# Two transformer layers on one core: scaled copies of V made for eight heads at a time, weights kept for the last queries, one residual sum in the tail moved to TensorE, and a new order of the work

## The chip, the core and the metric

The kernel runs on one core of one Trainium2 chip. The metric is the time of one execution on the device in microseconds (us). Engines are named as in the profile: PE is TensorE, ACT is ScalarE, DVE is VectorE, POOL is GpSimd, and SP is SyncE, which here only issues DMAs.

## What is computed

Two layers on x, 2048 tokens by 512 features, bfloat16. Each layer is attention (32 heads of 16) and a feed-forward block (hidden width 1792), both with a layer norm without weights in front and a residual sum behind.

```python
x = x + _A_ref(_layernorm(x), A_wqkv, A_wo)      # softmax(q k^T / 4) v, then @ wo
x = x + _B_ref(_layernorm(x), B_w1, ..., B_b2)   # gelu(h @ w1 + b1) @ w2 + b2
x = x + _A_ref(_layernorm(x), A_wqkv, A_wo)      # the same weights again
x = x + _B_ref(_layernorm(x), B_w1, ..., B_b2)
```

## The kernel before

**Cells and passes.** Queries are cut into four chunks of 512 columns (`segs`; in the second layer the last chunk is cut into two segments of 256), keys into 16 tiles of 128 (`kt`). A *cell* is one head, one key tile and 512 queries (or two heads with 256 queries each): one score matmul on PE (L1336), the exponential of a 128x512 PSUM bank, and a product with V (L1851). There are 4096 cells, 2048 per layer. A *pass* (`passes`) is one query segment, four heads (eight for the segments of 256) and a range of key tiles; over all 16 tiles it has 64 cells. Layer 2 begins with passes over key tiles 0 to 11 alone, since the last four tiles are not there yet.

**Two ways to an exponential.** Most cells go to ACT, two or three banks in one instruction (`exps`, L1787), and their result is one operand of V's product. Cells whose key tile is in `KD[l]` (five of the 16 tiles of a layer) may go to DVE instead: `dfirst` (L1493) makes an integer from the score that, read as bfloat16, is a rough exponential, and `dchain` (L1610 on POOL, L1615 and L1621 on DVE) makes three shifted versions of it. All four are multiplied with V and three scaled copies of V, tile `VC`, and the sum is a good exponential. `vcopies` (L1267, POOL) makes the copies, for all 32 heads of a key tile at a time, 15 instructions per layer; those of the second layer start when the first pass of that layer is reached.

**The layer norm and the feed-forward block.** `ln` and `ln_tile` compute statistics on DVE, the reciprocal root on POOL (L751), the normed tile on POOL (L767, into a ring `XLN` of two buffers), and SP transposes it by DMA (L771) into `XF`, for W1, or `XP`, for the next layer's projections. `hpair` is W1 (L638), `gelu` runs on ACT (L1077), `ytile` is W2. `wo` is the output projection; its result is added to x on DVE (L960). Weights stream through a ring `WR` of four buffers (`wloads`, `wload`, SP, L1012). `wlate` loads four W1 pieces of the very last segment into room that layer 1's keys had. For the last query chunk, W2 stays in the room of Q (`lent_q`).

**Lent room.** Exponentials wait for PE in the units `pt`: a ring of 15 and, when they are free, the rooms of K, Q, G, XP and V. The room's old keys are given as written each time a unit in it is written again (`pkeys`, `alias`; `over` for the buffers of DVE).

**The order.** Nothing of the order is written by hand. While the kernel is built, `_Sched` plays all threads against durations written in the code and emits, for each engine, a fixed list of instructions with semaphore waits. `_Op` carries an engine, a duration, what it reads and writes, and a priority (small is first). Rows of settings (`ROWS`), one for each of 160 stretches of the cells (`PIECES`), steer the choices. Where the plan has PE idle it puts in matmuls without use (`filler`, L1324); an empty column of a V product gets a product with zeros (L1859). On the chip each engine goes through its list in order and cannot change it.

The planner's line that decides between ready operations of one engine:

```python
ch = min(nowc, key=lambda c: (self._prio(c[0].op), c[0].seq))
```

Of the kernel before, what the change touches and what calls it, by code (L numbers as in the profile page):

```python
# [23 lines left out]
PT_RING = 15  # L24
# [3 lines left out]
W_MORE = 4  # L28
XT = 8
XLN_RING = 2  # L30
# [15 lines left out]
KD = ((4, 5, 6, 7, 8), (0, 1, 2, 12, 13))  # L46
# [9 lines left out]
QUEUE = 4  # L56
NAMES = ("SWAP", "SLACK", "LATE", "TOL", "BACKLOG", "OPENING", "TAIL", "PVP", "PTURG", "DUURG", "DULOW", "DWIDE", "RWIDE", "PTLOW", "FPRIO", "MID",
         "EVAC", "ROUNDS", "ALONE", "AHEAD", "PSHIFT", "QUEUE", "SOLO", "BACK", "SIDE", "BOTH", "DMAX", "GMAX", "PMORE", "DUMORE",)
ROWS = (
# [568 lines left out]
class _Plan:  # L628
# [336 lines left out]
    def wdone(self, piece, r):  # L965
        self.wleft[piece] -= 1
        if self.wleft[piece] == 0:
            yield ("rel", "w", r)
# [994 lines left out]
```

## Time and profile before

| what | value |
|---|---|
| median of 3 runs | 1505.63 us (1504.88 to 1507.16) |
| the profiled execution | 1504.69 us, span of its instructions 1502.9 us, so 1.8 us lie around the span |
| busy | ACT 1454.3 us (97%), PE 1443.9 (96%), DVE 1346.3 (90%), POOL 918.4 (61%) |
| granted TensorE clock | 1.00 throughout |
| exponentials on ACT (L1787) | 984 instructions over two banks, 342 over three |
| cells on DVE (L1493) | 1102 |
| scaled copies (L1267) | 30, 19.8 us of POOL, mean 662 ns |
| last exponential ends | 1471.5 us, that is 31.4 us before the end of the span |

A busy share is an average. PE's contains matmuls without use, and its durations overlap, since a matmul starts before the one ahead of it has ended. ACT's instructions overlap a little as well: two in a row start closer to each other than one lasts.

### The profile page before, as it was taken

The numbers are of one execution on the slowest core, as the hardware profiler recorded it, in microseconds if no ns is written. First come the engines' busy times: TensorE is split into PE (matmuls) and PEld (weight loads), VectorE is DVE, ScalarE is ACT, GpSimd is POOL, SyncE is SP. The second block draws the span as 40 slices with busy tenths as digits, with TensorE's granted clock in tenths as the row PEclk, the third lists the DMA queues.
The fourth block names the chain that finished last, engine by engine and source line by source line (L and its number), as shares of the span: only waits on it lengthen the run. The fifth ranks groups of instructions, "written<-read, shape, count | busy, mean of one in ns | idle before, by whom it ended". The sixth has DMA issues, their size and how long they took to land.

```text
span 1502.9 us, 46561 instructions
## 1 busy us (share of the span) xinstructions
PE 1443.9 (96%) x20102; PEld 440.9 (29%) x20102; DVE 1346.3 (90%) x2343; ACT 1454.3 (97%) x1385; POOL 918.4 (61%) x975
## 2 busy tenths in 40 slices
PE   8999999999999999999999999989999999999998
PEld 2222222222222222222222222222222222344345
DVE  5589999989999899998889788899989998999894
ACT  7999999999999999999889999999999999999994
POOL 4547766786655565645654456676766776676550
PEclk9999999999999999999999999999999999999999
DMA  5200001153021342114331441001144114411433
GB/s 148 51 1 2 1 12 34 36 156 92 23 51 37 107 111 64 47 37 127 93 99 41 144 113 30 9 2 44 30 118 130 29 37 135 146 26 44 136 100 108
DMA packets 145048, 103.41 MB, mean 69 GB/s; under 512 B 37069, under 2 KB 143822, under 8 KB 144846
## 3 DMA queue, kind: packets, MB, share of 16 engines
q1 hardware_dynamic: 144846, 100.44, 23.7%
q8 instruction: 161, 2.64, 0.7%
q14 instruction: 41, 0.34, 0.1%
HBM read 88.61 MB, written 4.19 MB: 62 GB/s over the span
## 4 chain that ended last, share of the span: by engine, by line
ACT 43%; PE 39%; DVE 16%; issue 1%; DMA 0%; POOL 0%; SPq 0%; ACTq 0%; DVEq 0%
ACT pt L1787 34%; PE ps L1851 13%; PE ps L638 13%; PE ps L1336 13%; DVE du L1493 6%; DVE du L1615 3%; ACT g L1077 3%; ACT kt L1787 2%; ACT v L1787 1%; ACT g L1787 1%; DVE kt L1493 1%; DVE v L1493 1%; ACT xp L1787 1%; PE ps L1324 1%; DVE stats L744 1%
## 5 line engine op out<-in xcount | busy, mean ns | idle before, releaser
L1787 ACT ACTIVATE pt<-ps 128x1024 bf16<-128x1024 f32 (+1 forms) x1122 | 1166.3, 1164 | 16.8 <-PE ps L1336 12.5
L1610 POOL TENSOR_SCALAR du<-du 128x1024 uint16<-128x1024 uint16 x430 | 446.9, 1043 | 300.7 <-DVE du L1493 159.0
L1493 DVE TENSOR_SCALAR du<-ps 128x512 uint16<-128x512 f32 x855 | 566.2, 682 | 55.4 <-PE ps L1336 50.6
L1336 PE MATMUL ps<-qp,kt 32*128 32x512 bf16 x4096 | 547.8, 384 | 27.6 <-ACT pt L1787 13.4
L1851 PE MATMUL ps<-pt,v 128*17 128x512 bf16 (+1 forms) x2795 | 384.4, 359 | 6.4 <-ACT pt L1787 1.6
L1851 PE MATMUL ps<-du,vc 128*17 128x512 bf16 (+1 forms) x2883 | 347.4, 357 | 2.5 <-DVE du L1615 1.6
L1336 PEld LDWEIGHTS ps<-qp,kt 32*128 32x128 bf16 x4096 | 140.9, 91 | 577.3 <-ACT pt L1787 172.4
L1615 DVE TENSOR_SCALAR du<-du 128x2048 uint16<-128x2048 uint16 (+1 forms) x313 | 226.1, 738 | 9.4 <-POOL du L1610 9.2
L1851 PE MATMUL ps<-du,v 128*17 128x512 bf16 (+1 forms) x961 | 159.2, 359 | 5.1 <-DVE du L1615 1.2
L1859 PE MATMUL ps<-vc,zero 128*17 128x512 bf16 x733 | 151.2, 381 | 0.0
L638 PE MATMUL ps<-xf,wr 128*32 128x512 bf16 (+1 forms) x1888 | 128.8, 365 | 1.0 <-DVE g L1056 0.9
L1623 POOL TENSOR_SCALAR du<-du 128x1024 uint16<-128x1024 uint16 x117 | 122.7, 1049 | 8.1 <-DVE du L1621 5.1
L1851 PEld LDWEIGHTS ps<-pt,v 128*17 128x17 bf16 x2795 | 93.6, 88 | 101.8 <-issue 63.9
L1493 DVE TENSOR_SCALAR kt<-ps 128x512 uint16<-128x512 f32 x167 | 113.6, 682 | 8.8 <-PE ps L1336 6.1
L638 PE MATMUL ps<-wr,g 128*32 128x512 bf16 x1600 | 119.8, 383 | 1.5 <-DVE du L1493 0.5
L1610 POOL TENSOR_SCALAR kt<-kt 128x1024 uint16<-128x1024 uint16 x84 | 87.7, 1045 | 52.4 <-DVE du L1615 25.6
L1284 POOL TENSOR_SCALAR qp<-q,mask 128x512 bf16<-128x512 bf16 (+1 forms) x91 | 64.0, 703 | 87.4 <-PE ps L1336 41.3
L1851 PEld LDWEIGHTS ps<-du,vc 128*17 128x17 bf16 x2883 | 94.2, 89 | 74.8 <-issue 45.0
L1851 PE MATMUL ps<-kt,vc 128*17 128x512 bf16 (+1 forms) x621 | 103.2, 339 | 0.1
L1787 ACT ACTIVATE kt<-ps 128x1024 bf16<-128x1024 f32 (+1 forms) x77 | 94.4, 1242 | 1.1 <-PE ps L1336 0.3
L1851 PE MATMUL ps<-kt,v 128*17 128x512 bf16 (+1 forms) x393 | 92.2, 360 | 1.4 <-DVE v L909 0.4
L1056 DVE TENSOR_SCALAR g<-ps,hb1t 128x512 bf16<-128x512 f32 (+1 forms) x112 | 78.9, 708 | 5.5 <-PE ps L638 5.0
(107 smaller groups left out, 1635.1 us busy)
## 6 DMA issues: line engine op xcount, KB each, us to landing
wr<-in_B_w_dram SPq DMA_DIRECT2D x256, 256.0 KB, 2.9
wr<-in_A_wqkv_dram SPq DMA_DIRECT2D x24, 256.0 KB, 2.9
wr<-in_A_wo_dram SPq DMA_DIRECT2D x18, 256.0 KB, 3.2
x<-in_A_x_dram SPq DMA_DIRECT2D x7, 512.0 KB, 4.2
kept<-x SPq DMA_DIRECT2D x4, 512.0 KB, 3.9
x<-kept SPq DMA_DIRECT2D x4, 512.0 KB, 4.1
out_dram<-x SPq DMA_DIRECT2D x16, 128.0 KB, 2.3
g<-in_A_wqkv_dram SPq DMA_DIRECT2D x3, 512.0 KB, 6.0
```

The source lines that it names most:

```text
L638: return [lambda e, a=a: e.matmul(out[32 * a:32 * a + 32, :], lhsT=lhsT[:, 32 * a:32 * a + 32], rhs=rhs, start=start, stop=stop, tile_posi ...
L1056: yield _Op("dve", 0.21 + n / 966, lambda e, fc=fc, pb=pb: e.tensor_scalar(T["G"][:, fc, q], pb, T["HB1T"][:, fc:fc + 1], None, op0=ALU.ad ...
L1077: lambda e, g=g: e.activation(out=g, in_=g, func=ACT.Gelu_apprx_tanh), reads=gk, writes=gk, prio=2)
L1284: yield _Op("pool", 0.27 + 0.42 * w / 512, lambda e, s=s, q=q, i=i, t=t, w=w: e.tensor_scalar(T["QP"][:, s, w * i:w * i + w], q, T["MASK"] ...
L1336: return (lambda e: e.matmul(o, lhsT=lhsT, rhs=rhs, start=True, stop=True, tile_position=(32 * a, 0)), ["K%d.%d.%d" % (l, gb, kt // 4), "Q ...
L1493: yield _Op("dve", 0.682, lambda e: e.tensor_scalar(u, self.bank(b), E_SCALE, E_BIAS, op0=ALU.mult, op1=ALU.add), reads=["B.%d" % b], writ ...
L1610: one = _Op("pool", 0.15 + 0.45 * n, lambda e, a=a, b=b: e.tensor_scalar(b, a, float(SHIFT), 1.0, op0=ALU.add, op1=ALU.mult), reads=key[0] ...
L1615: two = _Op("dve", 0.152 + 0.266 * n, lambda e: e.tensor_scalar(U[:, 2:4, 0:n, :], U[:, 0:2, 0:n, :], 2 * SHIFT, None, op0=ALU.add), reads ...
L1623: more = _Op("pool", 0.15 + 0.45 * n, lambda e, a=a, c=c: e.tensor_scalar(c, a, float(2 * SHIFT), 1.0, op0=ALU.add, op1=ALU.mult), reads=k ...
L1787: yield _Op("act", 0.065 + 0.4267 * n, lambda e, src=src, dst=dst: e.activation(out=dst, in_=src, func=ACT.Exp, scale=0.25), reads=["B.%d" ...
L1851: op.fns.append(lambda e, o=o, lhsT=q[0][0][m], rhs=q[0][1][:, n * m:n * m + n], a=a, st=st, sp=sp: e.matmul(o, lhsT=lhsT, rhs=rhs, start= ...
L1859: op.fns.append(lambda e, o=self.bank(b)[32 * a:32 * a + 17, :], rhs=rhs, a=a, st=not begun[a], sp=end: e.matmul(o, lhsT=T["ZERO"][:, 0:17 ...
```

## The change

- `KD` of the second layer is (1, 4, 7, 10, 13) in place of (0, 1, 2, 12, 13), so that it has one step. `VC` becomes two buffers, each for eight heads and five key tiles. A *visit* is a run of passes with the same eight heads, segment and key tiles; for each, `vcopies` issues three instructions over all its key tiles. A buffer is written again when the products of the visit that used it are past.
- The room set free goes to `PT_RING` (15 to 21) and `XLN_RING` (2 to 4).
- XP is no longer lent to exponentials. It becomes two weight buffers, in which Wo stays for the last three segments (`wkeep`); the four late W1 pieces are asked for 80 cells before the end (`WSOON`).
- W2 kept in the room of Q serves the last two query chunks, not only the last.
- Old keys of lent room are given as written at the first write alone (`once`).
- In the last segment x is added by a matmul with the identity into the bank of `wo`; the statistics read that bank, and ACT copies it to x. The bias of W2 is put into the bank first there.
- The norm into XP has priority 3.5 (`LNQ`), where the copies have 4 and it had 7. DMA transposes get priority 1.
- `GMAX` is gone, there are 61 rows of settings and another `PIECES`, and a stretch ends at a rounded place. Matmuls without use read `B2row` in place of `VC`.

```diff
-KD = ((4, 5, 6, 7, 8), (0, 1, 2, 12, 13))
+KD = ((4, 5, 6, 7, 8), (1, 4, 7, 10, 13))
...
+        T["WR"] += [T["XP"][:, 2 * i:2 * i + 2, :].rearrange("p c q -> p (c q)") for i in range(W_KEEP)]
-        T["VC"] = sb([128, NKD, 3, H * 17], BF16, "vc")
+        T["VC"] = sb([128, 2, 3, NKD, H // 4 * 17], BF16, "vc")
...
     def wo(self, l, seg, t):
+        if (l, seg) == (NL - 1, self.segs[l][-1]):
+            yield ("need", "exps")
+            b = yield ("acq", "misc")
+            yield self.resid(b, t, True, False)
...
+        if last:
+            yield ("give", ("xready", t, 2 * l + 1), b)
+            yield ("need", ("st", t))
+            yield _Op("act", 0.48, lambda e: e.copy(T["X"][:, t % XT, :], pb), ...)
+            yield ("give", ("xback", t))
+            return
+    def resid(self, b, t, start, stop):
+        return _Op("pe", MM, self.quads(self.bank(b), self.T["IDENT"], self.T["X"][:, t % XT, :], start, stop), ...)
...
     def wlate(self, todo):
+        yield ("cond", lambda: self.scored >= self.total - WSOON)
...
+    def wkeep(self, todo):
+        for i, (piece, (src, n), uses) in enumerate(todo):
+            if i < W_KEEP:
+                yield from self.wload(piece, src, n, uses, W_RING + W_MORE + i, ["XP.%d" % j for j in range(4)] if i == 0 else [])
+            else:
+                self.wleft[piece] = uses
+                yield ("give", ("w",) + piece, W_RING + W_MORE + i % W_KEEP)
...
     def ytile(self, l, seg, t):
-        tail = l == NL - 1 and seg[0] == self.NQ - 1
+        tail = l == NL - 1 and seg[0] >= self.NQ - 2
+        if l == NL - 1 and seg[0] == self.NQ - 1:
+            yield ("need", "exps")
...
-                yield ("spawn", self.ln(ts, xp, pk, LNP, gate=("pfree",) + prev if prev else None), LNP)
+                yield ("spawn", self.ln(ts, xp, pk, LNQ, gate=("pfree",) + prev if prev else None), LNQ)
...
     def vcopies(self):
+        for v in range(len(first)):
+            l, seg, g, kts = self.pas[first[v]][:4]
+            js = [j for j, kt in enumerate(KD[l]) if kt in kts]
+            if js:
+                if used[v % 2] is not None:
+                    yield ("cond", lambda pi=first[used[v % 2] + 1]: self.pv >= pi)
...
+                for i, w in enumerate(VW):
+                    yield _Op("pool", 0.15 + 0.133 * len(js), lambda e, i=i, w=w, v=v, js=js, src=src: e.tensor_scalar(
+                        T["VC"][:, v % 2, i, js[0]:js[-1] + 1, :], src, w, 1.0, op0=ALU.mult, op1=ALU.mult), ...)
...
     def dfirst(self, pair, j, b):
-                  reads=["B.%d" % b], writes=["DU.%d.0.%d" % (pair["du"], j)] + self.over(pair["du"]))
+                  reads=["B.%d" % b], writes=["DU.%d.0.%d" % (pair["du"], j)] + self.once.pop(("du", pair["du"], j), []))
...
     def exps(self):
-                reads=["B.%d" % b for b in self.slots[sl][:n]], writes=[k for r in run for k in self.pkeys(r)])
+                reads=["B.%d" % b for b in self.slots[sl][:n]], writes=[k for r in run for k in self.pkeys(r) + self.once.pop(r, [])])
```

How many instructions of each kind the two programs hold, counted in their built lists:

| | before | after |
|---|---|---|
| ACT exponentials over 1, 2 and 3 banks | 0, 984, 342 | 1, 976, 349 |
| cells on DVE | 1102 | 1096 |
| POOL shifted versions (two cells each; L1610, L1623) | 708 | 668 |
| DVE shifted versions, double (L1615) and single (L1621) | 388, 160 | 422, 123 |
| POOL scaled copies: 544 wide; 680; 136 | 30; 0; 0 | 18; 90; 18 |
| PE products with V over 512 columns, the zeros included | 7569 | 7477 |
| PE matmuls without use (128x512 bank, four at a time) | 516 | 516 |
| PE matmuls behind the last score, of W1's 256-column kind | 368 | 224 |
| DMA loads of W2 pieces and of Wo pieces into WR | 197, 18 | 169, 10 (and 2 into XP) |

More of the change, by code (lines that the diff above doesn't have):

```diff
@@ L742, in ln @@
         for t in tiles:
-            yield ("need", ("xready", t, self.phase[t // 4]))
-            yield _Op("dve", 0.66, lambda e, t=t: e.bn_stats(T["STATS"][:, t, :], T["X"][:, t % XT, :]),
-                      reads=["X.%d" % (t % XT)], writes=["ST.%d" % t])
+            b = yield ("need", ("xready", t, self.phase[t // 4]))
+            src, key = (self.bank(b), "B.%d" % b) if quick and self.phase[t // 4] else (T["X"][:, t % XT, :], "X.%d" % (t % XT))
+            yield _Op("dve", 0.66, lambda e, t=t, src=src: e.bn_stats(T["STATS"][:, t, :], src), reads=[key], writes=["ST.%d" % t], prio=prio)
+            if key[0] == "B":
+                yield ("give", ("st", t))
+                yield ("need", ("xback", t))
+                yield ("rel", "misc", b)
             yield _Op("dve", 0.17, lambda e, t=t: e.bn_aggr(T["MV"][:, t, :], T["STATS"][:, t, :]),
@@ L984, in first, with kept @@
             return [((l, seg, "O", j), rows(hbm["wo"], 256 * j, 0, D), seg[2] // 128) for j in range(2)]
+        def kept(l, seg):
+            return l == NL - 1 and seg[0] > 0
+        yield ("spawn", self.wkeep([x for o in order if kept(*o) for x in first(*o)]), 3)
         out = first(*order[0])
@@ L988, in wloads @@
             todo = [((l, seg, "1", p), cols(hbm["w1"], 256 * p), 2) for p in range(NFC // 2)]
-            tail = l == NL - 1 and seg[0] == self.NQ - 1
-            if not tail:
+            if l == NL - 1 and seg[0] == self.NQ - 2:
+                p = NFC // 2 - 1
+                todo.append(((l, self.segs[l][-1], "2", p), rows(hbm["w2"], 256 * p, 0, D), 8))
+            elif l < NL - 1 or seg[0] < self.NQ - 1:
                 todo += [((l, seg, "2", (t, p)), rows(hbm["w2"], 256 * p, 0, D), 1) for t in self.tiles(seg) for p in range(NFC // 2)]
             elif i == len(order) - 1:
-                p = NFC // 2 - 1
-                todo.insert(0, ((l, seg, "2", p), rows(hbm["w2"], 256 * p, 0, D), 4))
-                late = todo[1:1 + W_MORE]
-                del todo[1:1 + W_MORE]
-            if i < len(order) - 1:
+                late = todo[:W_MORE]
+                del todo[:W_MORE]
+            if i < len(order) - 1 and not kept(*order[i + 1]):
                 todo += first(*order[i + 1])
@@ L1004, in wloads @@
         for i, (piece, (src, n), uses) in enumerate(out):
-            if i == len(out) - (NFC // 2 + 1 - W_MORE):
-                yield ("spawn", self.wlate(late), 3)
+            if i == 0:
+                yield ("spawn", self.wlate([x for x in late]), 3)
             w = yield ("acq", "w")
@@ L1019, in wlate @@
         for i, (piece, (src, n), uses) in enumerate(todo):
-            yield from self.wload(piece, src, n, uses, W_RING + i, over)
+            yield from self.wload(piece, src, n, uses, W_RING + i, over if i == 0 else [])
+    def wkeep(self, todo):
+        for c in range(self.NQ):
+            for kind in "KVQ":
+                for i in range(4):
+                    yield ("need", (kind, 1, 4 * c + i if kind == "V" else i, c))
+        for i, (piece, (src, n), uses) in enumerate(todo):
[4 more added lines that the diff above has]
+                yield ("give", ("w",) + piece, W_RING + W_MORE + i % W_KEEP)
     def gkeys(self, seg, fs):
@@ L1082, in ytile @@
         T = self.T
-        tail = l == NL - 1 and seg[0] == self.NQ - 1
+        tail = l == NL - 1 and seg[0] >= self.NQ - 2
         last = NFC // 2 - 1
-        for p in range(1 if tail else NFC // 2):
-            yield ("need", ("g", l, seg, p))
+        if l == NL - 1 and seg[0] == self.NQ - 1:
+            yield ("need", "exps")
+        else:
+            for p in range(1 if tail else NFC // 2):
+                yield ("need", ("g", l, seg, p))
         b = None if tail else (yield ("need", ("w", l, seg, "2", (t, 0))))
@@ L1101, in ytile @@
             for j in range(2):
-                fns += self.quads(pb, T["G"][:, 2 * p + j, q], ws[j], p + j == 0, False)
-            if p == last:
+                fns += self.quads(pb, T["G"][:, 2 * p + j, q], ws[j], not early and p + j == 0, early and 2 * p + j == NFC - 1)
+            if p == last and not early:
                 fns += self.quads(pb, T["ONES1"][:, :], T["B2row"][:, :], False, True)
@@ L1234, in setup_attention @@
                 self.pvleft[(pi, a)] = len(kts)
+        self.visit = []
+        for pi, (l, seg, g, kts, part, final) in enumerate(self.pas):
+            new = pi == 0 or self.pas[pi - 1][0:2] != (l, seg) or self.pas[pi - 1][3:] != (kts, part, final) or self.heads(*self.pas[pi - 1][1:3])[0] != self.heads(seg, g)[0]
+            self.visit.append(self.visit[-1] + new if pi else 0)
         self.total, self.scored, self.nd, self.pa, self.pv = n, 0, 0, 0, 0
@@ L1250, in setup_attention @@
                      ["K0.%d.%d" % (i, c) for i in (0, 1) for c in range(self.NQ)] + ["PART1.%d" % g for g in range(4)]]
+        for du in range(self.own, len(self.cap)):
+            for j in range(self.cap[du]):
+                self.once[("du", du, j)] = self.over(du)
         self.lead = [min(pi for pi, p in enumerate(self.pas) if p[0] == l) for l in range(NL)]
@@ L1668, in setup_units @@
             for i in range(NDC):
-                self.alias[lo + i] = ["K1.%d.%d" % (i, c)] + ["XL.%d" % t for t in range(4 * c, 4 * c + 4)]
+                self.alias[lo + i] = ["K1.%d.%d" % (i, c)]
+                self.once[lo + i] = ["XL.%d" % t for t in range(4 * c, 4 * c + 4)]
         self.qblocks = len(self.blocks)
@@ L1722, in lent_g @@
                     yield ("need", ("xready", t, 2 * l + 2))
-    def lent_xp(self, lo, hi):
-        for c in range(self.NQ):
-            for kind in "KVQ":
-                for i in range(4):
-                    yield ("need", (kind, 1, 4 * c + i if kind == "V" else i, c))
-        for u in range(lo, hi):
-            yield ("rel", "pt", u)
     def lent(self, c, lo, hi):
```

88 lines of the change are left out of this document (50 added, 38 removed), and 119 rows, old and new, of tables (PIECES, ROWS).

## Prediction

> **What bounds the kernel now.** I read the page's busy line first, then ACT's waits, then stretches of time, then the two places where ACT stands still.
>
> ```profile
> span 1502.9 us, 46561 instructions
> PE 1443.9 (96%) x20102; PEld 440.9 (29%) x20102; DVE 1346.3 (90%) x2343; ACT 1454.3 (97%) x1385; POOL 918.4 (61%) x975
> ...
> PEld ps L1336 <- ACT pt L1787: 172.4, 383, 1.7
> ...
> ACT pt L1787 <- PE ps L1336: 12.5, 14, 7.8
> ```
>
> ACT and PE are both nearly full. The lower lines are of the table of waits (waiter, releaser, total us, times, longest): PE's weight loads for scores waited 172.4 us for ACT's exponentials to leave a bank, ACT waited 12.5 us for scores. So ACT sets the pace, with PE little behind. The table of stretches says where ACT is not busy (columns: PE, PEld, DVE, ACT, POOL busy, then clock and DMA):
>
> ```profile
> 100.00:700.00 600.00, 581.54 (x7541) 160.00 (x7537) 574.86 (x981) 596.10 (x566) 384.32 (x396) 1.00 0.20 56
> 700.00:800.00 100.00, 95.81 (x1312) 28.59 (x1309) 88.31 (x157) 90.30 (x88) 61.08 (x69) 1.00 0.33 91
> 800.00:1450.00 650.00, 624.32 (x8947) 194.67 (x8944) 593.65 (x1023) 644.89 (x606) 417.59 (x433) 1.00 0.26 75
> ...
> 1471.00:1503.00 32.00, 27.86 (x694) 18.59 (x682) 12.33 (x31) 11.89 (x19) 1.23 (x2) 1.00 0.37 110
> ```
>
> Outside the opening ACT misses 9.7 us between 700 and 800, some 9 us in 1250 us elsewhere, and it is a guest in the tail, where PE has 27.9 of 32. Three terms follow: ACT's work, the hole at 746, the tail.
>
> **ACT's work: +2.5 us.** From the list of built instructions: 8 exponentials fewer over two banks, 7 more over three, one over a single bank (six cells went from DVE to ACT). By the rows of shapes these take 1066 and 1493 ns; the copy of one bank (L834) 649 to 674, which I take as 0.6. -8 x 1.066 + 7 x 1.493 + 0.6 = +2.5. All are on ACT's path.
>
> **The hole at the layers' border: -6.1 us.** Timelines of ACT, POOL and SP there (start, us until the last of the row ends, instructions, [idle before]):
>
> ```profile
> 737.92 8.22 ACT L1787 ACTIVATE pt<-ps 128x1536 bf16<-128x1536 f32 x7
> 753.97 6.69 ACT L1787 ACTIVATE pt<-ps 128x1024 bf16<-128x1024 f32 x7 [7.82 <-PE ps L1336]
> ...
> 738.06 1.51 POOL L767 TENSOR_SCALAR xln<-x,rstd,nmr 128x512 bf16<-128x512 bf16 x2
> 739.80 1.37 POOL L1267 TENSOR_SCALAR vc<-v 128x544 bf16<-128x544 bf16 x2 [0.23 <-PE ps L1859]
> 741.53 4.98 POOL L1267 TENSOR_SCALAR vc<-v 128x544 bf16<-128x544 bf16 x7 [0.36 <-DVE ott L923]
> 746.61 1.52 POOL L767 TENSOR_SCALAR xln<-x,rstd,nmr 128x512 bf16<-128x512 bf16 x2
> ...
> 738.85 11.06 SPq L771 DMA_TRANSPOSE xp<-xln  x4
> ```
>
> ACT ends an exponential at 746.15 and waits 7.82 us for a score. That score needs a K tile whose projection PE starts at 751.64, when the transposes into XP are there; those need four normed tiles on POOL. POOL makes two, then nine scaled copies, then the other two at 746.61; `XLN` has two buffers. In the new list POOL's four L767 of this place stand together, directly behind the root, with four buffers, and the copies behind them. So the second pair is ready at 739.6 + 1.5 = 741.1 instead of 748.1. Two transposes take about 2.5 us of SP (the row of two at 753.78 says 2.50): the first pair is through at 741.3, the second at 743.8 instead of 749.9, 6.1 us earlier. Projection, cast, score and exponential move along, the first exponential to 747.9. 1.7 us of the hole stay. Next late is then PE: it has to put the output projections of the last segment (L638, 741.5 to 749.4) around it, in whose gaps it now runs 60 matmuls without use (L1324). In the new list PE has 16 and 4 of those around this border where it had 72 and 8: a sign that the gap is gone, not proof. Ends: 0 (another input of that score was as late) and -7.8.
>
> **The tail: -3.5 us.** The last exponential ends at 1471.46, the span 31.4 us later. Rows of PE and the last one of DVE:
>
> ```profile
> 1472.80 3.02 PE L638 MATMUL ps<-xf,wr 128*32 128x256 bf16 x104
> 1475.64 1.47 PE L638 MATMUL ps<-q,g 128*32 128x512 bf16 x24
> ...
> 1500.06 0.69 DVE L1109 TENSOR_TENSOR x<-x,ps 128x512 bf16<-128x512 bf16 x1 [1.25 <-PE ps L638]
> ```
>
> PE is the chain here from 1472.8 to 1500.0. 104 matmuls of W1 (256 columns) take 2.84 us until the next row, 27 ns each; of 512 columns, 24 take 1.29, 54 ns each. Behind the last score the new list has 144 fewer of the first kind: W1 of the segment before the last is now done ahead. -144 x 0.0273 = -3.9. Eight identity matmuls are new: +0.4. W2, Wo, the bias and W1 of the last segment are as many as before. The sum left, 22 us, can be packed like this: products with V end about 0.9 us after the last exponential (1.5 today, with 0.9 of W1 among them); DVE's norm of the heads takes 0.72 + 0.24 + 0.49 + 0.43 by its rows, so Wo starts at 3.0; the first half of gelu, which has 1.28 of table load and 1.70 ahead of it, is there at 3.0 too. From there 21.1 us of PE, 0.3 to 1 of waits, 0.75 for the last sum and 2.15 from there to the end of the span as today: 27.3 to 28, against 31.4. I take 27.9. The new cover: today W1 hides the norm and gelu; when it is gone PE idles about 1.1 us, which is in this sum. The old sum of x and `wo` on DVE (0.68 a tile) leaves the chain to the statistics; it was off PE's path, so nothing is counted. The bounds are 0 (all of it turns into waits) and -5.
>
> What leaves the tail lands before it: 3.9 us more of W1 on PE while ACT works. It is paid by 92 fewer products with V over 512 columns (77 of them zeros, the fewer cells on DVE the rest): 23 rounds of four at 0.215, -4.9. PE's main part is as long as before.
>
> **Everything else: -1.3 us.** Old keys waited for once can only take waits away. ACT's on PE's products (L1859 1.9, L1851 0.8) are 2.7 in total; I take half. Scaled copies: 18 of 544, 90 of 680, 18 of 136 columns. The row says 662 ns for 544; for 680 I scale to 0.83, between that and 1.05 (1024 columns, L1610); for 136 I take 0.3, between 0.29 (L648, 128 columns) and 0.49 (L1284, 256). 11.9 + 74.7 + 5.4 = 92 us for 19.8; 40 shifted versions fewer give back 42. POOL has 30 us more, 948 of about 1495, and waits for DVE most of its idle time (159.0 us for L1493 alone), so it hides. DVE: 6 cells less (-4.1), 34 doubles more at 0.743 (+25), 37 singles less at 0.49 (-18): +3 of 1346. SP: 36 loads fewer; ACT never waits for one. Room for `pt` is 21 + 0 against 15 + 4 with XP: no loss. Transposes now go ahead of weight loads; none of the longest 41 rows of the table of waits is for a weight load.
>
> **Sum.** 1504.69 + 2.5 - 6.1 - 3.5 - 1.3 = 1496.3; I say 1496, from the profiled execution, which lies 0.9 under the median of the three runs.
>
> **Rivals.** (a) *The hole stays*, because another input is late: V's copies of layer 2 now need key tile 10, whose V is projected after K of the third chunk, so DVE has no cells for the first 50 or so of the layer, and ACT takes them as scores come. For: DVE had cells at once with tiles 0 to 2. Against: ACT's share of cells is in the list already. Time 1496 + 6 = 1502.
>
> (b) *Slower: the copies hold up DVE's chains.* They come in threes, 2.5 us of POOL, 42 times, where they came twice per kernel. A shifted version behind them is that late, its buffer and its products too. Cells on DVE come every 1471 / 1102 = 1.34 us, so five own buffers of two cells cover 13.4 us; a pair needs 2 x 0.68 + 1.05 + 0.74 = 3.2 us and its products. It decides once a pair lives over 13.4 - 2.5 = 11 us. If each of 42 threes then cost ACT 0.4 us: +17, 1513. Against: POOL waits for DVE (159.0 us), hardly the reverse (DVE L1615 waited 9.2 us for POOL). [...]
>
> (c) *Better: the new order also takes the small waits.* In the timeline two-bank exponentials start 0.92 us apart at best (four from 1439.81 to 1443.50), 1.07 in the next run (eight from 1447.71 to 1456.27): ACT waited within what counts as busy. Over all 984 such starts this is up to 44 us, hole included. A fifth less gives 1488. For: fewer rounds of products. Against: a plan may as well make a fifth more, 1504, which the range has.
>
> (d) *The clock drops in the tail.* Today PE runs 16 matmuls without use there, the new list none. The row: 1.00 in every stretch, idle 0.8 us at most in the tail. If a pause let the clock fall, 21 us of PE would go at half pace, as the first L1324 of the opening do (nine in 4.02 us, 0.45 for 128 rows; four quarters of that, 32 rows each, now take 0.21 together): up to 1496 + 21 = 1517, for one short spell about 1499. [...]
>
> **How the numbers follow.** Forecast 0.55, (a) 0.15, (b) 0.13, (c) 0.15, (d) 0.02. The range takes in (a), most of (c) and the bounds of the hole and the tail, and the fifth more of small waits: 1486 to 1508. A measurement tells 0.2% (3 us) from no change: under 1502.6 counts as faster than the median. Faster: 0.55 x 0.96 + half of (a) + (c) = 0.75; same: 0.02 + half of (a) + a little of (b) = 0.11; slower 0.14.
>
> **What would show it.** ACT's longest wait for L1336 under 3 us; 31.4 us between last exponential and end become 28; L1267's successor (680 columns) at 0.7 to 0.9 us; ACT's exponentials 976 and 349 with unchanged means. I am wrong if a new wait over 4 us stands on ACT, if the mean of the two-bank row rises from 1066 (20 ns are 20 us), or if DVE's double rows wait for POOL.

## The result and the profile after

The changed kernel takes 1490.23 us (1489.52 to 1493.48, four runs) against 1505.89 (1504.88 to 1507.16, four runs) of the kernel before on the same chip: 15.7 us less, ratio 0.990, 95% interval 0.9883 to 0.9917. Forecast were 1496 and -9.6. The profiled execution took 1490.43 us, so 14.3 less than the profiled one before. The page after:

```profile
span 1488.6 us, 46274 instructions
...
PE 1432.6 (96%) x20012; PEld 436.7 (29%) x20012; DVE 1353.7 (91%) x2332; ACT 1457.6 (98%) x1387; POOL 942.6 (63%) x1032
```

ACT's longest wait for scores (table of waits; total, times, longest) was 7.8 us and is now 0.5:

```profile
ACT pt L1853 <- PE ps L1413: 6.1, 25, 0.5
```

The stretches, columns as before (PE, PEld, DVE, ACT, POOL, clock, DMA):

```profile
700.00:800.00 100.00, 94.98 (x1262) 27.38 (x1258) 83.11 (x142) 98.34 (x90) 59.60 (x64) 1.00 0.32 85
800.00:1450.00 650.00, 626.71 (x9154) 198.09 (x9146) 619.46 (x1058) 646.82 (x612) 431.85 (x476) 1.00 0.23 65
1462.00:1489.00 27.00, 23.76 (x563) 14.64 (x555) 7.76 (x20) 12.41 (x21) 1.09 (x2) 1.00 0.10 31
```

ACT misses 1.7 us between 700 and 800 where it missed 9.7. The last exponential ends at 1462.1 instead of 1471.5 (-9.35), and the tail behind it lasts 26.5 us instead of 31.4 (-4.9).

ACT's part of it can be split by taking the distance from the start of each exponential to the start of the next instruction, which also shows waits that the busy time hides. A two-bank exponential takes 0.904 us at best (the fastest tenth), a three-bank one 1.330. What is above these is waiting, and it is put down to what ended the wait by the trace.

| term | forecast | measured |
|---|---|---|
| ACT's number of cells (2994 to 3000) | +2.5 | +2.7 |
| the hole at the layers' border | -6.1 | -7.8 |
| ACT waiting for products with V (4.3 to 0.5 us) | -1.3 | -3.8 |
| ACT waiting for its own exponential directly ahead (3.1 to 0 us) | 0 | -3.1 |
| other, as the difference | 0 | +2.6 |
| tail | -3.5 | -4.9 |

The row of own exponentials is of waits that the table of waits does not list: such an exponential starts 0.09 us after the end of the one ahead of it, where others start before that end, and about 0.25 us above the best distance. There are 12 in the trace of the kernel before and none after; in the built lists a semaphore wait of ACT on itself stands ahead of 16 exponentials before and of one after. Most of the rest, +2.6, is in small waits for scores (without the hole 27.9 us before, 30.8 after).

At the border, the timeline of the changed kernel (ACT, PE, SP) has no hole:

```profile
729.70 28.38 ACT L1853 ACTIVATE pt<-ps 128x1536 bf16<-128x1536 f32 x22
...
736.96 1.05 PE L653 MATMUL ps<-xp,wr 128*32 128x512 bf16 x16
...
746.06 0.62 PE L653 MATMUL ps<-wr,otn 128*32 128x512 bf16 x8 [0.56 <-DVE kt L853]
...
730.81 2.51 SPq L790 DMA_TRANSPOSE xp<-xln  x2
```

The last transpose leaves SP's queue at 733.3, its data are in XP at 734.5, and PE runs the projections out of XP (`xp`, from 736.96) ahead of the output projections (`otn`, from 746.06). Before it was the other way round, as the kernel before's row of PE for the last of its output projections and for the first projection says:

```profile
748.39 1.05 PE L638 MATMUL ps<-wr,otn 128*32 128x512 bf16 x16 [0.36 <-DVE x L960]
...
751.64 1.04 PE L638 MATMUL ps<-xp,wr 128*32 128x512 bf16 x16
```

### The profile page after: what moved, and what is told of

Read it like the earlier page. It is cut to its first block, busy times and chain, and to the rows that moved or that the text cites. A ratio compares the mean times of both kernels' runs of the same rounds, so it can differ in the third digit from the quotient of the medians.

```text
span 1488.6 us, 46274 instructions
## 1 busy us (share of the span) xinstructions
PE 1432.6 (96%) x20012; PEld 436.7 (29%) x20012; DVE 1353.7 (91%) x2332; ACT 1457.6 (98%) x1387; POOL 942.6 (63%) x1032
## 4 chain that ended last, share of the span: by engine, by line
ACT 49%; PE 37%; DVE 12%; POOL 1%; DMA 1%; issue 1%; SPq 0%
ACT pt L1853 42%; PE ps L653 12%; PE ps L1413 12%; PE ps L1917 12%; DVE du L1570 5%; ACT g L1128 3%; DVE du L1692 2%; DVE kt L1570 1%; ACT kt L1853 1%; ACT q L1853 1%; ACT L1128 1%; PE ps L1401 1%; DVE x L1167 1%; ACT L1853 1%; DVE g L1107 0%
## 5 line engine op out<-in xcount | busy, mean ns | idle before, releaser
L1853 ACT ACTIVATE pt<-ps 128x1024 bf16<-128x1024 f32 (+1 forms) x1253 | 1306.9, 1177 | 8.0 <-PE ps L1413 6.1
L1687 POOL TENSOR_SCALAR du<-du 128x1024 uint16<-128x1024 uint16 (+1 forms) x429 | 445.8, 1044 | 232.4 <-DVE du L1570 97.4
L1692 DVE TENSOR_SCALAR du<-du 128x2048 uint16<-128x2048 uint16 x336 | 245.4, 744 | 4.2 <-POOL du L1687 4.2
L1925 PE MATMUL ps<-b2row,zero 128*17 128x512 bf16 x788 | 145.5, 381 | 0.0
L1570 DVE TENSOR_SCALAR kt<-ps 128x512 uint16<-128x512 f32 x165 | 109.9, 681 | 10.5 <-PE ps L1413 9.7
L653 PE MATMUL ps<-wr,g 128*32 128x512 bf16 x1408 | 105.0, 383 | 1.1 <-DMA wr<-in_B_w_dram 0.5
L1342 POOL TENSOR_SCALAR vc<-v 128x680 bf16<-128x680 bf16 (+2 forms) x126 | 87.4, 693 | 25.4 <-DVE du L1692 8.2
L1700 POOL TENSOR_SCALAR du<-du 128x1024 uint16<-128x1024 uint16 (+1 forms) x93 | 97.1, 1044 | 8.4 <-DVE du L1692 4.4
L1917 PE MATMUL ps<-kt,vc 128*17 128x512 bf16 (+1 forms) x615 | 96.0, 339 | 1.2 <-DVE kt L1692 0.8
L786 POOL TENSOR_SCALAR xln<-x,rstd,nmr 128x512 bf16<-128x512 bf16 x58 | 47.0, 818 | 21.9 <-DVE du L1692 10.9
```

What stands on the lines that cost most here:

```text
L653: return [lambda e, a=a: e.matmul(out[32 * a:32 * a + 32, :], lhsT=lhsT[:, 32 * a:32 * a + 32], rhs=rhs, start=start, stop=stop, tile_posi ...
L1342: yield _Op("pool", 0.15 + 0.133 * len(js), lambda e, i=i, w=w, v=v, js=js, src=src: e.tensor_scalar(T["VC"][:, v % 2, i, js[0]:js[-1] + 1 ...
L1570: yield _Op("dve", 0.682, lambda e: e.tensor_scalar(u, self.bank(b), E_SCALE, E_BIAS, op0=ALU.mult, op1=ALU.add), reads=["B.%d" % b], writ ...
L1687: one = _Op("pool", 0.15 + 0.45 * n, lambda e, a=a, b=b: e.tensor_scalar(b, a, float(SHIFT), 1.0, op0=ALU.add, op1=ALU.mult), reads=key[0] ...
L1692: two = _Op("dve", 0.152 + 0.266 * n, lambda e: e.tensor_scalar(U[:, 2:4, 0:n, :], U[:, 0:2, 0:n, :], 2 * SHIFT, None, op0=ALU.add), reads ...
L1700: more = _Op("pool", 0.15 + 0.45 * n, lambda e, a=a, c=c: e.tensor_scalar(c, a, float(2 * SHIFT), 1.0, op0=ALU.add, op1=ALU.mult), reads=k ...
```

## The experiments

One thing holds for all of them: an edit makes the planner write another list from the place where it first matters, and the chosen rows of settings no longer fit there. So a single total mixes the edit with a new list. I therefore give the cell up to which the list is unchanged, and read the place in question in the trace.

**1. Old and new code, each with plain and with both choices of rows** (four kernels).

```diff
-PIECES = (0, 29, 0, 45, ...)
+PIECES = (0,) * 160          # old_plain, new_plain
```

In `old_code_new_rows` and `new_code_old_rows` `NAMES`, `ROWS` and `PIECES` are exchanged.

> The kernel before with the first row of its settings in all 160 places, so that no place has a row chosen for it. It gives the first corner of a table: old code and new code, each with plain and with chosen rows. Theory 1 (the parts of the change earn the time by themselves): old and new code lie as far apart with plain rows as with chosen ones, 12 to 18 us. Theory 2 (the new choice of rows earns it): with plain rows they lie within 5 us of each other. What the chosen rows are worth to the old code I can only bound: 0 to 40 us, so 1506 to 1546 us.

> The changed kernel with the first row of its settings in all 160 places. Theory 1: 12 to 18 us under the old code with plain rows. Theory 2: within 5 us of it. For the tail alone (from the end of the last exponential to the end) both theories agree, as rows choose little there: 26 to 28 us here against 30 to 32 in the old code with plain rows. For the hole at the layers' border: if the code takes it away (the norm that goes ahead, four buffers for its tiles), it is under 2 us here and over 5 us in the old code with plain rows.

> The kernel before with the changed kernel's rows and their places: a choice of rows made for other code. Theory 1 gives at or above the old code with plain rows, since the choice does not fit. Theory 2 in a strong form (the rows carry the gain to any code) gives under 1500 us; in the weak form (the rows earn it only for the code that they were chosen on) again about the plain time, so only the strong form is told apart here: above 1506 us refutes it.

> The changed kernel with the rows of the kernel before and their places. If rows fit only the code that they were chosen on, this lies within 6 us of the changed kernel with plain rows. If the old rows carry over, it lies some 10 us or more under it. Its tail should be 26 to 28 us whatever the rows, if the tail's gain is made by the code alone.

| rows | old code | new code | difference |
|---|---|---|---|
| each its own | 1505.9 | 1490.2 | -15.7 |
| plain | 1517.6 | 1499.2 | -18.4 |
| those of before | 1505.9 | 1509.8 | +3.9 |
| those of after | 1537.0 | 1490.2 | -46.8 |

(Against the kernel before: old plain 1.0076, interval 1.0061 to 1.0091; new plain 0.9953, 0.9938 to 0.9968; old code with new rows 1.0207, 1.019 to 1.0224; new code with old rows 1.0024, 1.0014 to 1.0034.) Theory 1 holds: without any chosen rows the code is worth as much as with them (18.4 us; 12 to 18 were expected). Rows fit only the code that they were chosen on; they are worth 11.7 us to the old code and 9.0 to the new one, and with rows of the other code each is slower than with plain ones, by 19.4 and 10.6. The tail is 25.9 and 26.0 us in the new code with plain and with old rows, 33.0 and 38.4 in the old code with plain and with new ones: the short tail comes with the code, and in the old code its length depends on the rows as well. Three expectations failed. The old code's tail with plain rows was to be 30 to 32 us. The new code with old rows was to lie within 6 us of the one with plain rows and is 10.6 above it. And with plain rows the old code has no hole at the border, its longest wait between 700 and 900 us is under 0.6. So the hole belonged to one choice of rows, and the code's gain of 18.4 contains none of it. Of these 18.4, 7.1 are the tail. In the main part, by starts, ACT's waits for products went from 12.3 to 1.7 us and those for the exponential directly ahead from 8.0 (31 times) to 1.5 (6 times), while waits for scores grew from 28.2 to 31.2 and ACT got 9 cells more.

**2. The hole: the copies moved behind both pairs of tiles.** List unchanged up to cell 2057.

```diff
             yield ("cond", lambda l=l: self.pv >= self.lead[l])
+            if l:
+                yield ("need", ("K", 1, 0, 2))
```

> The kernel before with one edit: the nine scaled copies of the second layer that stand on GpSimd between the two pairs of normed tiles wait until the third chunk's first projection of K is done, so they go behind both pairs. The order is the same up to cell 2057, just at the hole of 7.8 us. Theory 1 (the prediction: the copies delay the second pair by 6.1 us, and with it the key tile that ScalarE's exponential waits for): ScalarE's longest wait there is 1.2 to 2.5 us, and the first exponential behind it starts 5 to 6.5 us earlier. Theory 2 (two buffers for the normed tiles, or the norm that starts only when the second chunk's last projection is done at 734 us, make the hole): the second pair still waits for the transposes of the first and the hole is over 4.5 us. What this does to the total is a matter of the new order behind it, so I only expect 1498 to 1510 us.

Measured 1517.0 us (ratio 1.0074, 1.0059 to 1.0089). ACT, PE, POOL and SP at the place:

```profile
752.87 6.88 ACT L1789 ACTIVATE pt<-ps 128x1536 bf16<-128x1536 f32 x6 [7.13 <-PE ps L1338]
...
747.28 1.05 PE L638 MATMUL ps<-wr,otn 128*32 128x512 bf16 x16 [0.36 <-DVE x L960]
...
749.22 1.05 PE L638 MATMUL ps<-xp,wr 128*32 128x512 bf16 x16
752.10 0.40 PE L1326 MATMUL ps<-vc,zero 128*17 128x512 bf16 x4 [1.83 <-POOL vc L1269]
...
738.51 5.82 SPq L771 DMA_TRANSPOSE xp<-xln  x4
```

The second pair of tiles was normed from 741.0 and the last transpose left SP's queue at 744.3, as the prediction wanted it (741.1 and 743.8). By the trace its data landed at 747.1, where they landed at 751.2 in the kernel before. The hole shrank by 0.7, to 7.13 us, and the exponential came 1.1 earlier. PE was busy with the 64 matmuls of the output projection until 748.3, tile after tile, the later ones waiting for DVE to empty the bank (L960), and only then came the projection. Some 1.8 us more are of the edit's own making: a product with zeros reads `VC` and waited for the moved copies. Even without that the hole would be over 5 us. Theory 1 is refuted. Theory 2 gave the size. Of its two reasons, the two buffers did make POOL wait for the first pair's transposes (1.8 and 0.6 us), but the tiles had landed 1.2 us before PE was free. The other reason, a norm that starts only behind the second chunk's last projection at 734, is left as it was by this edit.

**3. The hole: the order on PE.** Old code, plain rows in one stretch; list unchanged up to cell 1679.

```diff
-PIECES[64:84] = (0, 33, 42, 42, 0, 30, 0, 32, 3, 0, 10, 0, 23, 0, 27, 40, 0, 1, 1, 18)
+PIECES[64:84] = (0,) * 20
```

> The kernel before with one stretch of its settings changed: from cell 1638 to 2150 it has the first row, as in the old code with plain rows, which shows no hole at the border. The order is the same up to cell 1679. In its list the projections of the third chunk for layer 2 (cells 2034 to 2079) stand ahead of the output projections of the last segment of layer 1 (2082), where before they stand behind them (2060 to 2069 against 2069 to 2099). Theory 1 (that order on TensorE makes the hole, not the copies): no wait of ScalarE over 2 us between cells 2000 and 2150, with nine copies on GpSimd as before. Theory 2 (the copies make it): a wait over 4 us stays. The total is a matter of what else that row does, 1498 to 1510.

Measured 1516.2 us (1.0067, 1.0052 to 1.0083). The timeline there:

```profile
757.21 18.42 ACT L1783 ACTIVATE pt<-ps 128x1536 bf16<-128x1536 f32 x17 [1.91 <-PE ps L1847]
...
721.78 1.03 PE L634 MATMUL ps<-xp,wr 128*32 128x512 bf16 x16
...
736.12 0.62 PE L634 MATMUL ps<-xp,wr 128*32 128x512 bf16 x8
...
759.78 0.61 PE L634 MATMUL ps<-wr,otn 128*32 128x512 bf16 x8 [0.24 <-DVE v L845]
...
755.45 1.37 POOL L1263 TENSOR_SCALAR vc<-v 128x544 bf16<-128x544 bf16 x2 [11.76 <-PE ps L1855]
```

The projections go ahead of the output projections, and the longest wait is 1.9 us, for products and not for scores, as theory 1 has it. But two other things moved with that order. The last 16 projections of the second chunk, behind which XP may be written again, come at 721.8, where the kernel before has them here:

```profile
734.33 1.05 PE L638 MATMUL ps<-xp,wr 128*32 128x512 bf16 x16
```

So all four transposes have landed at 734.5 instead of 751.2. And the copies, nine as before, now stand behind both pairs of tiles (from 755.45). Experiment 2 had the copies there too and kept its hole, so they are not enough; which of the two places in PE's order it takes is not separated. Nothing of the change is in this kernel. That it is 10 us slower in total comes from other places (it is 8 us late at the last cell, and its tail lasts 35.7): removing the hole alone is not worth 7.8 us when the rows around it change. As to the norm's new priority: with `LNQ = 7` the changed kernel's list is the same up to cell 2368, beyond the border, so that edit does not set this order either. That was read from the list; it was not run.

**4. The tail's residual on DVE again.** List unchanged to the last score.

```diff
-            b = yield ("acq", "misc")
-            yield self.resid(b, t, True, False)
...
-            yield _Op("act", 0.48, lambda e: e.copy(T["X"][:, t % XT, :], pb), ...)
-            yield ("give", ("xback", t))
-            return
```

> The changed kernel with the tail's residual taken back: in the last segment VectorE adds x to the output projection in the bank, as before, and the eight identity matmuls go; the order of the instructions is the same up to the last score. So everything up to the end of the last exponential should take the same time within 0.5 us, and only the tail (26.5 us) can move. Theory 1 (the prediction: the sum is off the path of TensorE): the tail is 26.1 to 26.6 us, the eight identity matmuls being 0.4 of it. Theory 2 (the sum stands on the chain from the output projection to the normed tiles, where TensorE has nothing else left): each half of the segment is late by one or two sums of 0.68 us, and the tail is 27.2 to 28.0 us, the kernel 0.7 to 1.5 us slower.

Measured 1488.76 us (0.9885, 0.987 to 0.99), the tail 26.3 us. Theory 1. This kernel is not told apart from the changed one, whose interval overlaps; of the 1.9 us between the two profiled executions 1.7 lie ahead of the last exponential's end, with the same instructions, where 0.5 was expected. The chain did become shorter by the change: the first normed half starts 6.7 us behind the last exponential instead of 8.0, and W1 starts 9.6 behind it instead of 10.2. But PE had the kept W2 of the segment before to do meanwhile, so its work sets the tail, and the identity matmuls add to that work (without them PE is busy 0.6 us less in the tail and waits 0.4 for gelu):

```profile
1471.70 3.23 PE L653 MATMUL ps<-xf,kt 128*32 128x256 bf16 x112
...
1485.15 0.60 PE L653 MATMUL ps<-wr,g 128*32 128x512 bf16 x8
```

(Changed kernel; W1 of the last segment and PE's last row.)

**5. and 6. Weights through the ring again.** Lists unchanged up to cell 3132. First Wo alone, then all three edits of the weights.

```diff
         def kept(l, seg):
-            return l == NL - 1 and seg[0] > 0
+            return False                                   # both
-        tail = l == NL - 1 and seg[0] >= self.NQ - 2
+        tail = l == NL - 1 and seg[0] == self.NQ - 1       # weights_streamed
-        yield ("cond", lambda: self.scored >= self.total - WSOON)   # weights_streamed
```

> The changed kernel without the kept weights: all pieces of Wo and W2 of the last segments go through the ring of four again, and the room of the second copy's slots stays unused. The order is the same up to about cell 3130 of 4096. Theory 1 (the prediction): the kept weights are what lets the 144 matmuls of W1 go ahead of the last score; without them these come back behind it, and the tail is 26.5 + 3.9 = 30.4 us, within 0.6; TensorE's row of 256 columns behind the last exponential is over 200 matmuls long against 112. Theory 2 (W1 goes ahead since the new settings or the later loads of W2 say so): the tail stays under 27.5 us, and only the transferred bytes go up by some 9 MB. The stretch between cell 3130 and the last exponential moves by no more than 3 us in either, TensorE having less to do there in theory 1.

> The changed kernel with all three of its weight edits undone: Wo and W2 of the last segments go through the ring of four again, W2 stays only for the last query chunk, and the four late W1 pieces are asked for as late as before. The room of XP stays unused. The run without the kept Wo alone left the tail at 26.5 us, so Wo is not what moves W1 ahead. In the list of this kernel 352 matmuls of W1 stand behind the last score, against 224 in the changed kernel and 368 before. Theory 1 (W1 is late because the ring of four is full of other weights; each of the three edits frees it, and they cover for each other): 128 x 0.0273 = 3.5 us come back, the tail is 29.5 to 30.5 us. Theory 2 (the tail got shorter by the statistics in the bank and the bias ahead, W1 only being pushed around): it stays under 28. For the main part: Wo alone cost 6 us between cells 3130 and 4095; if that is the price of the loads, it is 6 to 10 here; if it is the price of a list whose settings no longer fit, it can come out anywhere between 0 and 10.

Wo alone: 1497.2 us (0.9941, 0.9925 to 0.9958), tail 26.5: theory 2, it moves nothing in the tail. All three: 1497.5 us (0.9946, 0.9931 to 0.9961), tail 29.9: theory 1. Its matmuls of W1 ahead of the last segment's stand behind the last exponential again:

```profile
1467.96 2.80 PE L653 MATMUL ps<-xf,wr 128*32 128x256 bf16 x96
```

So keeping Wo alone makes nothing of the tail's 4.9 us, and the three together make 3.4, all of it work of PE (27.0 us busy behind the last exponential against 23.65, no pause in either). The kept W2 and the late pieces were not undone one at a time, so whether one of them does it, or they cover for each other, is not shown. The expected 3 us for the main part was exceeded by the first: its last exponential is 7.8 us late, of which 0.9 were there before the list changes. ACT waits for no weight in it; it has 959 two-bank and 365 three-bank exponentials, that is 3013 cells against 3000, and 13 x 0.452 = 5.9 us. The second has 3006 cells and is 3.5 late, of which 2.7 are cells. These are lists in which DVE got fewer cells, no price of the loads that I can show.

**7. Tiles for DVE.**

```diff
-KD = ((4, 5, 6, 7, 8), (0, 1, 2, 12, 13))      # old code, plain rows
+KD = ((4, 5, 6, 7, 8), (1, 4, 7, 10, 13))
```

> The kernel before with the first row of settings everywhere (1517.6 us) and, besides, the key tiles 1, 4, 7, 10, 13 for VectorE in the second layer in place of 0, 1, 2, 12, 13. Theory 1 (the tiles spread over the layer give VectorE more cells at its start, and that is the gain of cells 2048 to 2560): the second layer is 3 to 8 us shorter than with the old tiles, most of it in its first 500 cells, so 1510 to 1514 us. Theory 2 (VectorE's cells are paced by what its chains can take, whichever tiles they are): within 3 us of 1517.6.

Measured 1520.0 us (1.0097, 1.0082 to 1.0112), 2.4 above the old code with plain rows. It was 4.9 us ahead in cell 2560 and lost that again by cell 2816. Theory 2: by themselves the new tiles gain nothing that stays; they are what lets the copies be made with one step.

**8. The room that the copies set free.**

```diff
-PT_RING = 21                                   # new code, plain rows
+PT_RING = 15
```

> The changed kernel with the first row of settings everywhere and 15 units for the results of the exponentials in place of 21, so that the room that the smaller copies of V set free is unused. To be held against the changed kernel with that row everywhere (1499.2 us, last exponential at 1472.0) and the old code with it (1517.6 us, 1482.0). Theory 1 (the room is what the main part gains by: an exponential waits for a unit until its products are done): the last exponential 5 to 10 us later, 1504 to 1509 us, and ScalarE waits again for TensorE's products with V (5.7 us in the old code with plain rows, 1.1 in the new one). Theory 2 (the room is not short, as the prediction has it: 21 against 15 and 4 of XP is no loss and no gain): within 3 us of 1499.2.

Measured 1516.2 us (1.0068, 1.0053 to 1.0083): 17 us above the new code with plain rows, all but 0.6 of the main part's loss behind cell 2048, in the second layer. ACT's waits for products, first with 15 units, then with 21, then the old code with plain rows:

```profile
ACT pt L1849 <- PE ps L1913: 2.0, 4, 1.0
ACT kt L1849 <- PE ps L1913: 1.6, 1, 1.6
```

```profile
ACT pt L1849 <- PE ps L1913: 1.1, 1, 1.1
```

```profile
ACT pt L1783 <- PE ps L1847: 5.7, 3, 2.9
ACT kt L1783 <- PE ps L1847: 1.6, 3, 0.6
```

By starts these waits are 5.7, 1.7 and 12.3 us. Both have nearly the same number of cells on ACT (3022 and 3019), so this loss is waiting, not work: of two-bank exponentials alone 11.6 us more. But most of it is waiting for scores (40.2 us by starts against 31.2), not for products. The sign is theory 1's, its mechanism accounts for 4.0 of the 15.7 us by which the last exponential is later, and the size is beyond both. Nor is it a pure undoing: the list is another from cell 10 on, and the old code had 15 units and, late, four more in XP.

**9. Old keys at every write.**

```diff
-reads=..., writes=[k for r in run for k in self.pkeys(r) + self.once.pop(r, [])])
+reads=..., writes=[k for r in run for k in self.pkeys(r) + self.once.get(r, [])])
```

(The same in `dfirst`; new code, plain rows; list unchanged up to cell 508.)

> The changed kernel with the first row of settings everywhere and the old keys of lent room given at every write again, not only at the first. The prediction allowed 1.3 us for this edit. Theory 1 (waits of ScalarE that had no use are gone): 1 to 4 us above 1499.2, with ScalarE's waits for products up from 1.1 us. Theory 2 (the keys were long settled, the edit changes the list and nothing else): within 1 us if the list is the same, and anywhere within 4 us on either side if it is not, without more waits for products.

Measured 1509.4 us (1.0023, 1.0014 to 1.0033), 10 above the new code with plain rows; its waits for products are 6.6 us by starts against 1.7. That looks like theory 1, but 5.7 of the 6.6 stand ahead of writes into the ring (`pt`), whose units have no old keys. What the keys do themselves is to be seen in another wait: ACT waited 13 times for its exponential directly ahead, 3.5 us, where the other kernel did 6 times, 1.5 us. The units of one lent room share old keys, so a write to one unit waits for the write just ahead to another. The edit undoes only part, since the products do not name these keys again, as they did in the kernel before. The size is outside both theories, and on the way this list was 7.8 us ahead of the other (cell 768) and 12.9 behind (cell 1792). With one list each, the rest of the 10 us and the re-planning can't be separated; this part stays open.

## Why the prediction was right, and where it was not

**What bounds the kernel: right.** ACT's exponentials keep their price (1062 and 1499 ns against 1066 and 1493), and the time followed ACT's cells and waits, and the tail.

**ACT's work: right**, +2.7 for +2.5.

**The hole: the size about right by luck, the reason wrong.** The step that failed is "In the new list POOL's four L767 of this place stand together, directly behind the root": the four that stand together are XF's, a different norm. Those of XP come as two pairs, and in the changed kernel both are done at 731.5, before the border, so that PE can take the projections first. And in the kernel before, another input was nearly as late, which the prediction had as its end of 0: with the tiles in time the hole was still 7.1 us (experiment 2), for PE stood in the output projections. The prediction also took a transpose as through when it left SP's queue (749.9); its data landed at 751.2. I named the output projections as what is late next and then priced them as if they would yield. The hole goes when PE's order changes in two places, the second chunk's last projections and the third chunk's ahead of the output projections; this order needs nothing of the change (experiment 3), and which place is the one stays open.

**The tail: the mechanism right, a term mis-sized.** Behind the last exponential PE was busy 27.4 us and idle 1.15; after, 23.65 and 0.0. The busy part is -3.75 against the forecast's -3.9 + 0.4 = -3.5. The other 1.15 is the pause of "about 1.1 us" that I left in for the lost cover of W1. In the kernel before, 0.79 of it was a wait for a normed tile, with no W2 of the segment before left to do; now 24 matmuls of that W2 stand behind the first transposes of the tiles (from 1469.95) and the pause is gone. That W2 was in the room of Q before as well, and with the weights streamed again there is no pause either (experiment 6), so the kept weights are not the reason; why the list has it so stays open. The remark that the old sum was off PE's path holds in the new order (experiment 4). What moves the 144 matmuls was not said; undoing the three weight edits brings 128 of them back (experiment 6).

**Everything else: a term mis-sized, and one left out.** Waits for products were given half of 2.7; they went nearly altogether, 4.3 to 0.5 us by starts. The line "Room for `pt` is 21 + 0 against 15 + 4 with XP: no loss" is the likely place: XP was free only late, and with 15 units these waits come back in part (5.7 against 1.7 us, experiment 8, under a new list). The term left out is ACT's wait for its own exponential directly ahead, 3.1 us to 0. The prediction has its cause in "Old keys waited for once can only take waits away" but looked only at waits for PE; experiment 9 has 17 such waits in the built list against 6. Against both work the small waits for scores, 2.9 us more.

**Copies: right.**

```profile
L1342 POOL TENSOR_SCALAR vc<-v 128x680 bf16<-128x680 bf16 x90 | 69.0, 767 | 18.7 <-DVE du L1692 5.6 <-PE ps L1917 2.0 <-DVE v L868 1.9
```

767 ns for 680 columns (0.83 taken), 648 for 544, 373 for 136 (0.3 taken): 87.4 us in all for 92. POOL has 24 us more for 30, DVE 7 for 3.

**Rivals.** (a) does not show: ACT waits for no cell at the layer's start. (b) is refuted: DVE's double rows (L1692) waited 4.2 us for POOL against 9.2 before, with 24 us more on POOL, and took 748 ns each against 743, 2 us over 332 of them. (c) happened in part, with the waits for products and not with those for scores (27.9 us by starts without the hole, now 30.8). (d): the tail has 1.00 throughout. The 3 us in its "for one short spell about 1499" were my estimate and no run shows them; between runs at mean clocks of 1.000 and 0.999 the time grew by 1.2 us on average in the kernel before and by 1.7 in that of experiment 9 (last section).

## What to carry to other kernels

A wait at a boundary has every input of the waiting instruction behind it, and the order of a full engine is one of them: before pricing the removal of one late input, follow the next one on the engine that must run last (here PE) as if the first were already there. Where a planner writes the order, compare old and new code under the same neutral settings as well as under their own: a feature of the profile that vanishes with the settings, such as this hole, says little about the code. An engine can also wait for itself: 0.25 us at a time, in gaps too short for the table of waits, came to 3.1 us here, and 8.0 under plain rows. In a tail with enough ready work, count the work of the full engine; a shorter chain beside it gained nothing here (experiment 4: tail 26.5 us with it, 26.3 without).

## What the runs showed of the hardware

**In two profiled runs TensorE's clock was 0.50 for a spell, behind moments in which PE was about half busy.** In that of experiment 9 (mean clock 0.997) it fell in the middle of the kernel. Stretches of 1 us (columns as above):

```profile
1103.00:1104.00 1.00, 0.83 (x16) 0.21 (x8) 1.00 (x2) 1.00 (x1) 0.00 (x0) 1.00 0.27 93
1104.00:1105.00 1.00, 0.40 (x8) 0.14 (x8) 1.00 (x3) 1.00 (x1) 0.80 (x1) 1.00 0.00 0
1105.00:1106.00 1.00, 0.52 (x12) 0.11 (x8) 1.00 (x2) 1.00 (x2) 1.00 (x2) 1.00 0.00 0
1106.00:1107.00 1.00, 0.30 (x8) 0.00 (x0) 1.00 (x1) 1.00 (x1) 0.53 (x1) 0.94 0.00 0
1107.00:1108.00 1.00, 0.78 (x8) 0.14 (x8) 1.00 (x3) 1.00 (x1) 0.00 (x0) 0.50 0.00 0
```

PE was busy 2.05 of 4 us, its longest pause there 0.93 us, and then the clock was 0.50 until about 1117.1 (0.50 in the stretch from 1116 to 1117, 0.94 in the next); matmuls of 0.39 us took 0.59 to 0.64, and ACT waited 5.28 us for a score. The other is of experiment 1, the new code with plain rows (mean clock 0.999). The spell, with the 3.40 us ahead of it, in which PE was busy 1.64:

```profile
666.90:670.30 3.40, 1.64 (x25) 0.45 (x25) 3.40 (x5) 3.40 (x2) 1.69 (x2) 1.00 0.00 0
670.30:673.70 3.40, 3.40 (x29) 0.69 (x25) 1.67 (x4) 3.37 (x4) 0.43 (x1) 0.50 0.00 0
```

The profiled runs of the new code with old rows, of experiments 3, 7 and 8 and of Wo alone have a mean clock of 0.999 as well, the remaining ones 1.000, the kernel before and the changed one among them. Rival (d) went by the length of a pause, 0.8 us at most in the tail of the kernel before; ahead of experiment 9's spell the longest was 0.93 us, little more, with PE half busy. What makes the clock fall is not shown.

A lower mean clock went with a longer time. Each run on record has its mean clock, and in the same kernel the runs at 0.999 are longer on average than those at 1.000: in experiment 9 the means are 1510.2 us (four runs) and 1508.5 (five), and its run at 0.997, the profiled one, took 1513.1; for the kernel before beside it they are 1506.4 (six) and 1505.2 (seven). So in these two kernels a mean clock lower by 0.001 went with 1.7 and 1.2 us more.
